# Keeping 21 more rows of x in SBUF between the two passes of a channel-attention kernel

## The chip, the core and the metric

The kernel runs on one core of a Trainium2 chip. A core has TensorE (PE in the profile: matrix products), VectorE (DVE: element-wise work), ScalarE (ACT), GpSimd (POOL) and SyncE (SP), each with an instruction queue of its own. They share SBUF, the on-chip memory with 128 partitions, and PSUM, a small memory into which TensorE writes. Transfers between the chip's main memory (HBM) and SBUF are carried by 16 DMA engines. An engine issues a transfer from its queue and goes on; whoever needs the data waits on a semaphore.

The metric is the device time of one execution in microseconds. Before the change the median of three runs was 741.14 us (741.08 to 743.83).

## What is computed

The input `x` has 384 x 384 pixels with 384 channels in bfloat16, 113.2 MB. Every channel gets one factor, and the factor depends on all pixels:

```python
gap = jnp.mean(xf, 1)                 # xf: pixels x channels
gmp = jnp.amax(xf, 1)
h_a = relu(gap @ w1)                  # w1: 384 x 96
h_m = relu(gmp @ w1)
scale = sigmoid(h_a @ w2 + h_m @ w2)  # w2: 96 x 384
return x * scale                      # one factor per channel
```

So all of `x` has to be read before the first output can be made. What of `x` does not stay on the chip between the two passes has to be read a second time.

## The kernel before

**Rows.** The code counts `x` in rows. One row is one pixel on each of the 128 partitions: 128 x 384 x 2 bytes = 98,304 bytes, or 768 bytes per partition. There are 1152 rows (`TOT`). A block of n rows is n consecutive pixels per partition, so a transfer moves n x 768 consecutive bytes for each partition.

**Where rows live.** SBUF holds six slots of 44 rows (`SLOTS`, L17, tiles `x0` to `x5`) and an 11-row tile `acc`. Between the passes these rows of `x` stay on the chip: the 264 rows in the six slots at the end of the first pass, 16 rows that are copied into PSUM (`kept_ps`, L195) and 2 rows that are copied into another PSUM bank (`kept_b`, L197). The other rows are read again: 859 rows that passed through the slots, and 11 rows (L218, L225) that were loaded beside the 2 kept ones. 264 + 16 + 2 + 859 + 11 = 1152.

**First pass** (the loop at L170). SyncE issues the loads (L174), in the order of the list `loads` (L131 to L139): 16 rows into slot 0 as two transfers of 4 and 12 rows, 13 rows into slot 1, then the 25 blocks of `PASSING` (43, 44, 44, ... down to 13 rows; 859 in all), which go round the six slots beginning with slot 5, then the 264 rows that stay, in the 28 pieces of `STAYING`. That makes 56 transfers. A load into a slot waits until the block before it in that slot has been used by both of its readers. TensorE adds up the channels of each block by products with a column of ones (`sums`, L147). VectorE keeps a running maximum in `acc`, in instructions over 6 and 5 rows in turn (L190). After the first block VectorE copies 16 rows into PSUM (L195), and after the second 2 rows (L197).

**Between the passes.** A short serial chain on all engines folds the sums and maxima, multiplies them with the weights and ends in `scale_bc`, the 384 factors on every partition (L202 to L231).

**Second pass** (the loop at L284). For each block in `order` VectorE multiplies the block by the factors in place (`multiply`, L236) and ScalarE issues the store (L254). First come the six blocks that stayed, the first three of them in small pieces (`FIRST_STORES`), with the two stores of `acc` in between. Once a slot's store has landed, SyncE reads the next of the 20 `again` blocks into it (L263): 19 of 44 rows and, since the list is sorted by size, one of 23 rows at the end. The first two go out as five pieces and one. The two kept blocks come last (L296 to L299): they are multiplied out of PSUM into the slot of the sixth block from the end, and stored.

**Who sets the order.** Each engine works through its queue in order. In the second pass SyncE's order is as written (`manual_schedule`, L282). The order on the other engines is fixed when the program is compiled, by the order of the program text among the instructions whose inputs are there by then. ScalarE's queue is in that order too, so a store cannot overtake the one before it on that queue.

Of the kernel before, what the change touches and what calls it, by code (L numbers as in the profile page):

```python
# [11 lines left out]
BF16 = mybir.dt.bfloat16  # L12
# [3 lines left out]

SLOTS = (44, 44, 44, 44, 44, 44)  # L17
PSUM_ROWS = 16
BANK_ROWS = 2

FIRST_LOAD = 4
# [1 line left out]
ACC_ROWS = 11  # L23

PASSING = (
    43, 44, 44, 43, 43, 44, 43, 42, 42, 39, 38, 37, 36, 36, 35, 34, 32, 29, 29, 27, 27, 23, 21, 15, 13,
)
STAYING = (
    (19, 17, 8), (18, 16, 10), (16, 14, 14), (13, 11, 11, 9), (10, 9, 9, 8, 8), (6, 6, 5, 5, 5, 4, 4, 3, 3, 3),
)  # L30

FIRST_STORES = ((1, 2, 3, 4, 4, 6, 8, 8, 8), (8, 8, 9, 9, 10), (10, 12, 22))

# [9 lines left out]
def kernel(  # L43
# [7 lines left out]
    nc = tc.nc  # L51
    P = nc.NUM_PARTITIONS
    B_, H, W, C = x.shape
# [5 lines left out]
    NS = len(SLOTS)  # L59
# [3 lines left out]
    orr = out.rearrange("b h w c -> (b h w) c")  # L63

    def rows_of(ap, first, n):

        return ap[first * P:(first + n) * P, :].rearrange("(p n) c -> p n c", n=n)
# [4 lines left out]


    beside = BANK_ROWS + A
    head = PSUM_ROWS + beside
    n_stay = sum(SLOTS)
    n_pass = TOT - head - n_stay
    assert sum(PASSING) == n_pass
    stay = []
    for i, n in enumerate(SLOTS):  # L80
        stay.append([head + n_pass + sum(SLOTS[:i]), n, i])
    again = [(head, n_pass % SLOTS[0])] + [
        (head + n_pass % SLOTS[0] + SLOTS[0] * i, SLOTS[0]) for i in range(n_pass // SLOTS[0])
    ]


    small = consts.tile([P, 16], BF16)
# [20 lines left out]
    ]  # L108
    nc.scalar.activation(out=scale_bc[0:1, 0:1], in_=pick[0:1, 0:1], func=ACT.Sigmoid)  # L109
    acc = consts.tile([P, A, C], BF16)  # L110
    slots = [xpool.tile([P, n, C], BF16, name=f"x{s}") for s, n in enumerate(SLOTS)]


    bank_a = psum.tile([P, 512], F32)
    bank_b = psum.tile([P, 512], F32)
    kept_ps = psum.tile([P, PSUM_ROWS, C], BF16)
    sum_ps = bank_a[0:NQP, 0:MM_ROWS * P]
# [6 lines left out]
    z_ps = bank_a[:, 512 - C:512]  # L124
    kept_b = bank_b[:, 0:C * BANK_ROWS // 2].bitcast(BF16).rearrange("p (n c) -> p n c", n=BANK_ROWS)
    gsum_ps = bank_b[:, C:C + CQ]
# [1 line left out]

    loads = [(0, PSUM_ROWS, 0, 0, PSUM_ROWS), (PSUM_ROWS, beside, 1, 0, beside)]  # L131
    done = head
    for i, n in enumerate(PASSING):
        loads.append((done, n, (i - len(PASSING)) % NS, 0, n))
# [8 lines left out]
    def sums(rows, n, done, total):  # L143
        for k in range(0, n, MM_ROWS):
            g = min(MM_ROWS, n - k)
            for q in range(CQ):
                nc.tensor.matmul(  # L147
                    sum_ps[q * QP:q * QP + 1, 0:g * P],
                    lhsT=ones_bf[:, 0:1],
                    rhs=rows[:, k:k + g, q * P:(q + 1) * P],  # L150
                    start=(done + k == 0),
                    stop=(done + k + g == total),
                )

    def turn_sums():

        for r in range(MM_ROWS):
            nc.scalar.copy(out=s_sb[r % 2], in_=sum_ps[:, r * P:(r + 1) * P])  # L158
            nc.tensor.matmul(gsum_ps, lhsT=s_sb[r % 2], rhs=pick, start=(r == 0), stop=False)  # L159

    def tail_sums(rows, n, last):
        for k in range(n):
            for q in range(CQ):
                nc.tensor.matmul(  # L164
                    gsum_ps[:, q:q + 1], lhsT=rows[:, k, q * P:(q + 1) * P], rhs=ones_bf,
                    start=False, stop=(last and k == n - 1 and q == CQ - 1),
                )

    done = turn = 0
    for i, (first, n, s, lo, hi) in enumerate(loads):  # L170
        rows = slots[s][:, lo:hi, :]
        m = hi - lo
        for a, b in ((0, FIRST_LOAD), (FIRST_LOAD, m)) if i == 0 else ((0, m),):
            nc.sync.dma_start(out=rows[:, a:b, :], in_=rows_of(xr, first, n)[:, lo + a:lo + b, :])  # L174
        if i < n_loads - SUM_TAIL:
            sums(rows, m, done, TOT - tail_rows)
        else:
            tail_sums(rows, m, i == n_loads - 1)
        done += m
        if i == n_loads - SUM_TAIL - 1:  # L180
            turn_sums()
        if i == 0:
            nc.vector.tensor_copy(out=acc, in_=rows[:, 0:A, :])  # L183
            lo = A
        j = 0 if i else A
        while j < m:
            c, e = ACC_PARTS[turn]
            turn = (turn + 1) % len(ACC_PARTS)
            e = min(e, c + m - j)
            nc.vector.tensor_tensor(  # L190
                out=acc[:, c:e, :], in0=acc[:, c:e, :], in1=rows[:, j:j + e - c, :], op=ALU.max
            )
            j += e - c
        if i == 0:
            nc.vector.tensor_copy(out=kept_ps.bitcast(U32), in_=rows.bitcast(U32))  # L195
        elif i == 1:
            nc.vector.tensor_copy(out=kept_b.bitcast(U32), in_=rows[:, 0:BANK_ROWS, :].bitcast(U32))  # L197

# [7 lines left out]
    def acc_rows(ap, lo, hi):  # L206
        return rows_of(ap, PSUM_ROWS, beside)[:, BANK_ROWS + lo:BANK_ROWS + hi, :]

    n = A
    acc_pieces = []  # L210
    while n > 1:
# [5 lines left out]
        lo, hi = n, acc_pieces[0][0] if acc_pieces else A  # L217
        nc.sync.dma_start(out=acc[:, lo:hi, :], in_=acc_rows(xr, lo, hi))  # L218
        acc_pieces.append((lo, hi))
    for q0, part in tp_ps:  # L220
        n = part.shape[1]
# [12 lines left out]
    def multiply(dst, src):  # L234
        n = dst.shape[1]
        nc.vector.tensor_tensor(  # L236
            out=dst, in0=src, in1=scale_bc.unsqueeze(1).to_broadcast([P, n, C]), op=ALU.mult
        )
# [52 lines left out]
            read_into(order[k - 1][2])  # L291
    in_order.close()
    assert not again
    s = order[-NS][2]
    n = PSUM_ROWS + BANK_ROWS
    multiply(slots[s][:, 0:PSUM_ROWS, :], kept_ps)  # L296
    nc.scalar.dma_start(out=rows_of(orr, 0, PSUM_ROWS), in_=slots[s][:, 0:PSUM_ROWS, :])
    multiply(slots[s][:, PSUM_ROWS:n, :], kept_b)
    nc.scalar.dma_start(out=rows_of(orr, PSUM_ROWS, beside)[:, 0:BANK_ROWS, :], in_=slots[s][:, PSUM_ROWS:n, :])  # L299
# [28 lines left out]
```

## Time and profile before

| What | Value |
|---|---|
| median of the runs | 741.14 us (741.08, 741.14, 743.83) |
| span of the profiled execution | 743.3 us |
| bytes read and written | 198.92 MB and 113.25 MB |
| mean rate over the span | 420 GB/s |
| VectorE busy | 490.1 us (66%) |
| TensorE busy | 131.4 us (18%) |
| ScalarE and GpSimd busy | 3.3 us and 0.7 us |
| first pass, to the last maximum over x | to 270.7 us |
| first multiplication of the second pass | at 276.3 us |
| last instruction of VectorE | at 706.1 us |

The only time that is given for the profiled execution is its span, from the first to the last instruction; it lies 2.2 us (0.3%) above the median and within the three runs. A page of a profile shows busy time by engine, the span in 40 slices of 18.6 us, the DMA queues, the chain of waits that ended last, and groups of like instructions with what ended the idle time before them. DMA queue q1 carries what SyncE issues, q10 what ScalarE issues.

### The profile page before, as it was taken

Reading aid. Unit: us, or ns where it says so; the run is one execution under the profiler, and the core shown is the slowest. Engines: PE = TensorE matmul, PEld = TensorE weight load, DVE = VectorE, ACT = ScalarE, POOL = GpSimd, SP = SyncE. Lnnn points to the kernel's source line nnn. Section 1 sums busy time; section 2 is a strip of 40 time slices with the busy share of each in tenths; the row PEclk is TensorE's granted clock in tenths of the full one; section 3 lists DMA queues with packets and bytes.
Section 4 is the critical chain, followed back from the end, with each engine's and each line's share of the span. In section 5 each row is a group of like instructions: output and inputs, shape, how many; then the busy total and the mean of one; then the engine's idle time right before and its main releaser. Section 6 shows DMA issues by size and latency. Waiting matters only on the chain.

```text
span 743.3 us, 2595 instructions
## 1 busy us (share of the span) xinstructions
PE 131.4 (18%) x969; PEld 41.7 (6%) x969; DVE 490.1 (66%) x285; ACT 3.3 (0%) x9; POOL 0.7 (0%) x6
## 2 busy tenths in 40 slices
PE   1554445454544540000000000000000000000000
PEld 0111111111111120000000000000000000000000
DVE  5889999999999989998444433434444444433600
ACT  0000000000000000000000000000000000000000
POOL 0000000000000000000000000000000000000000
PEclk9866565567555555555555555555555555555555
DMA  9999999999999979999999999999999999999997
GB/s 381 436 427 432 432 428 431 424 424 438 417 426 420 414 256 376 427 433 433 433 429 435 435 429 433 433 435 435 429 429 429 435 433 436 435 435 427 425 435 310
DMA packets 18812, 312.33 MB, mean 420 GB/s; under 512 B 2448, under 2 KB 3056, under 8 KB 8304
## 3 DMA queue, kind: packets, MB, share of 16 engines
q1 hardware_dynamic: 12464, 198.92, 63.1%
q10 hardware_dynamic: 6336, 113.25, 35.7%
q8 instruction: 7, 0.11, 0.1%
q14 instruction: 5, 0.04, 0.0%
HBM read 198.92 MB, written 113.25 MB: 420 GB/s over the span
## 4 chain that ended last, share of the span: by engine, by line
another core or an unknown queue 40%; DMA 37%; DVE 15%; DVEq 1%; SPq 1%; issue 1%; PE 0%; ACT 0%; ACTq 0%
DMA x<-in_x_dram 31%; DVE acc L190 11%; DMA out_dram<-x 7%; DVE x L236 2%; DVEq L323 1%; SPq L263 1%; DVE kept_ps L195 0%; DVE acc L213 0%; DVE acc L236 0%; DVE acc L183 0%; PE bank_a L230 0%; ACT scale_bc L231 0%; SPq L174 0%; DVE bank_b L197 0%
## 5 line engine op out<-in xcount | busy, mean ns | idle before, releaser
L236 DVE TENSOR_TENSOR x<-x,scale_bc 128x16896 bf16<-128x16896 bf16 (+11 forms) x40 | 229.1, 5769 | 196.4 <-DMA x<-in_x_dram 195.2
L190 DVE TENSOR_TENSOR acc<-acc,x 128x2304 bf16<-128x2304 bf16 (+5 forms) x225 | 245.9, 1166 | 12.8 <-DMA x<-in_x_dram 12.6
L147 PE MATMUL bank_a<-x,small 128*1 128x512 bf16 (+3 forms) x912 | 126.6, 584 | 140.7 <-DMA x<-in_x_dram 140.7
L147 PEld LDWEIGHTS <-small 128*1 128x1 bf16 x912 | 37.8, 112 | 229.1 <-issue 227.6
L183 DVE COPY acc<-x 128x4224 bf16<-128x4224 bf16 x1 | 1.3, 1260 | 5.4 <-DMA x<-in_x_dram 5.4
L195 DVE COPY kept_ps<-x 128x3072 uint32<-128x3072 uint32 x1 | 3.4, 3354 | 0.0
L236 DVE TENSOR_TENSOR x<-kept_ps,scale_bc 128x6144 bf16<-128x6144 bf16 x1 | 3.4, 3351 | 0.0
L213 DVE TENSOR_TENSOR acc<-acc 128x384 bf16<-128x384 bf16 (+2 forms) x4 | 2.6, 658 | 0.1
L236 DVE TENSOR_TENSOR acc<-acc,scale_bc 128x1920 bf16<-128x1920 bf16 (+1 forms) x2 | 2.4, 1250 | 0.0
L158 ACT COPY w_sb<-bank_a 65x128 f32<-65x128 f32 x2 | 0.5, 262 | 265.7 <-PE bank_a L147 265.1
L164 PEld LDWEIGHTS <-x 128*128 128x128 bf16 x39 | 1.3, 109 | 0.0
L109 ACT ACT_TABLE_LOAD x1 | 1.3, 1283 | 0.7 <-PEq L312 0.7
L159 PE MATMUL bank_b<-small,w_sb 65*128 65x3 f32 x4 | 1.2, 365 | 0.4 <-ACT w_sb L158 0.4
L164 PE MATMUL bank_b<-small,x 128*128 128x1 bf16 x39 | 1.2, 165 | 0.0
L159 PE MATMUL bank_b<-small,scale_bc 65*128 65x3 f32 x4 | 1.1, 353 | 0.0
L159 PEld LDWEIGHTS bank_b<-small,w_sb 65*128 65x128 f32 x4 | 1.0, 313 | 0.9 <-ACT w_sb L158 0.9
L159 PEld LDWEIGHTS bank_b<-small,scale_bc 65*128 65x128 f32 x4 | 1.1, 323 | 0.0
L224 DVE TENSOR_REDUCE small<-bank_a 128x2 bf16<-128x256 bf16 x1 | 0.4, 427 | 0.6 <-PE bank_b L223 0.6
L223 PE MATMUL bank_a<-ident_bf,acc 128*128 128x128 bf16 x2 | 0.4, 300 | 1.8 <-DVE acc L213 1.8
L92 DVE MEMSET small<- 128x1 bf16 x1 | 0.1, 59 | 0.8 <-PEq L312 0.8
L118 DVE MEMSET bank_a<- 128x512 f32 x1 | 0.5, 485 | 0.1
L197 DVE COPY bank_b<-x 128x384 uint32<-128x384 uint32 x1 | 0.6, 554 | 0.0
(24 smaller groups left out, 6.3 us busy)
## 6 DMA issues: line engine op xcount, KB each, us to landing
out_dram<-x ACTq DMA_DIRECT2D x22, 4224.0 KB, 79.8
x<-in_x_dram SPq DMA_DIRECT2D x21, 4224.0 KB, 29.2
x<-in_x_dram SPq DMA_DIRECT2D x4, 4128.0 KB, 39.2
x<-in_x_dram SPq DMA_DIRECT2D x2, 4032.0 KB, 49.9
x<-in_x_dram SPq DMA_DIRECT2D x2, 3456.0 KB, 44.2
x<-in_x_dram SPq DMA_DIRECT2D x2, 2784.0 KB, 38.1
x<-in_x_dram SPq DMA_DIRECT2D x2, 2592.0 KB, 35.5
x<-in_x_dram SPq DMA_DIRECT2D x6, 768.0 KB, 16.0
```

The lines of the kernel that those rows point to most:

```text
L109: nc.scalar.activation(out=scale_bc[0:1, 0:1], in_=pick[0:1, 0:1], func=ACT.Sigmoid)
L147: nc.tensor.matmul(sum_ps[q * QP:q * QP + 1, 0:g * P], lhsT=ones_bf[:, 0:1], rhs=rows[:, k:k + g, q * P:(q + 1) * P], start=(done + k == 0 ...
L159: nc.tensor.matmul(gsum_ps, lhsT=s_sb[r % 2], rhs=pick, start=(r == 0), stop=False)
L164: nc.tensor.matmul(gsum_ps[:, q:q + 1], lhsT=rows[:, k, q * P:(q + 1) * P], rhs=ones_bf, start=False, stop=(last and k == n - 1 and q == C ...
L183: nc.vector.tensor_copy(out=acc, in_=rows[:, 0:A, :])
L190: nc.vector.tensor_tensor(out=acc[:, c:e, :], in0=acc[:, c:e, :], in1=rows[:, j:j + e - c, :], op=ALU.max)
L195: nc.vector.tensor_copy(out=kept_ps.bitcast(U32), in_=rows.bitcast(U32))
L197: nc.vector.tensor_copy(out=kept_b.bitcast(U32), in_=rows[:, 0:BANK_ROWS, :].bitcast(U32))
L213: nc.vector.tensor_tensor(out=acc[:, 0:h, :], in0=acc[:, 0:h, :], in1=acc[:, n - h:n, :], op=ALU.max)
L236: nc.vector.tensor_tensor(out=dst, in0=src, in1=scale_bc.unsqueeze(1).to_broadcast([P, n, C]), op=ALU.mult)
L263: nc.sync.dma_start(out=slots[s][:, j:j + m, :], in_=rows_of(xr, first, n)[:, j:j + m, :])
L323: with _tile.TileContext(nc) as tc:
```

## The change

[...] No transfer in this program is issued by GpSimd. [...]

- `held` is loaded as the third load of the first pass, summed and maximised like any block, and stays there.
- One block of 21 rows leaves `PASSING`, which now has 24 blocks and 838 rows. With 24 blocks the round through the slots begins at slot 0, and so the first two loads (16 and 13 rows) move from slots 0 and 1 to slots 4 and 5.
- The rows that are read again are now 18 blocks of 44 rows and two of 23 (`AGAIN`), still 20 blocks.
- After the second pass's loop `held` is multiplied in place and stored, ahead of the two blocks kept in PSUM.

```diff
+RING_BYTES = 256
+HELD_ROWS = 21
 PASSING = (
-    43, 44, 44, 43, 43, 44, 43, 42, 42, 39, 38, 37, 36, 36, 35, 34, 32, 29, 29, 27, 27, 23, 21, 15, 13,
+    43, 44, 44, 43, 43, 44, 43, 42, 42, 39, 38, 37, 36, 36, 35, 34, 32, 29, 29, 27, 27, 23, 15, 13,
 )
+AGAIN = (44,) * 18 + (23, 23)
...
-    head = PSUM_ROWS + beside
+    held_at = PSUM_ROWS + beside
+    head = held_at + HELD_ROWS
...
-    again = [(head, n_pass % SLOTS[0])] + [
-        (head + n_pass % SLOTS[0] + SLOTS[0] * i, SLOTS[0]) for i in range(n_pass // SLOTS[0])
-    ]
+    assert sum(AGAIN) == n_pass
+    again = [(head + sum(AGAIN[:i]), n) for i, n in enumerate(AGAIN)]
...
+    nc.dynamic_dma_scratch_size = RING_BYTES
+    nc.lookup_mloc("DynamicDMAScratchLoc").dims = [P, RING_BYTES]
+    held = nc.alloc_sbuf_tensor_at("held", [P, HELD_ROWS, C], BF16, offset=RING_BYTES).ap()
...
-    loads = [(0, PSUM_ROWS, 0, 0, PSUM_ROWS), (PSUM_ROWS, beside, 1, 0, beside)]
+    bufs = [*slots, held]
+    loads = [
+        (0, PSUM_ROWS, NS - 2, 0, PSUM_ROWS), (PSUM_ROWS, beside, NS - 1, 0, beside), (held_at, HELD_ROWS, NS, 0, HELD_ROWS),
+    ]
...
-        rows = slots[s][:, lo:hi, :]
+        rows = bufs[s][:, lo:hi, :]
...
     assert not again
+    multiply(held, held)
+    nc.scalar.dma_start(out=rows_of(orr, held_at, HELD_ROWS), in_=held)
```

## The prediction

> **What bounds the kernel now.** I read the page's head and slices first, then the DMA queues, the stretches of the two passes, the chain of waits and the waits of SyncE's queue. In the page, busy time comes before the slices:
>
> ```profile
> span 743.3 us, 2595 instructions
> ...
> PE 131.4 (18%) x969; PEld 41.7 (6%) x969; DVE 490.1 (66%) x285; ACT 3.3 (0%) x9; POOL 0.7 (0%) x6
> ...
> DVE  5889999999999989998444433434444444433600
> ...
> DMA  9999999999999979999999999999999999999997
> GB/s 381 436 427 432 432 428 431 424 424 438 417 426 420 414 256 376 427 433 433 433 429 435 435 429 433 433 435 435 429 429 429 435 433 436 435 435 427 425 435 310
> ```
>
> No engine is busy all the time, but the transfers are: 9 in every slice except at the boundary of the passes (slice 15) and at the end. The rate is the same for reads alone (slices 2 to 14), reads and writes together (17 to 36) and writes alone (38, 39). So the kernel is bound by bytes, whichever way they go. The queues:
>
> ```profile
> q1 hardware_dynamic: 12464, 198.92, 63.1%
> q10 hardware_dynamic: 6336, 113.25, 35.7%
> q8 instruction: 7, 0.11, 0.1%
> q14 instruction: 5, 0.04, 0.0%
> HBM read 198.92 MB, written 113.25 MB: 420 GB/s over the span
> ```
>
> All data go through two hardware queues, and there is no queue of GpSimd's. Stretches of the span (columns: window, its length, busy us of PE, PEld, DVE, ACT, POOL, clock of PE, DMA share, GB/s):
>
> ```profile
> 20.00:100.00 80.00, 37.37 (x267) 11.26 (x264) 74.33 (x65) 0.00 (x0) 0.00 (x0) 0.68 1.01 433
> ...
> 240.00:262.00 22.00, 11.95 (x90) 3.27 (x84) 21.82 (x23) 0.00 (x0) 0.00 (x0) 0.50 1.01 413
> ...
> 270.00:278.00 8.00, 2.44 (x36) 1.64 (x33) 5.88 (x13) 0.83 (x3) 0.00 (x0) 0.50 0.60 166
> ...
> 292.00:335.00 43.00, 0.00 (x0) 0.00 (x0) 43.00 (x10) 0.00 (x0) 0.00 (x0) 0.50 1.02 418
> 335.00:660.00 325.00, 0.00 (x0) 0.00 (x0) 149.97 (x17) 0.00 (x0) 0.00 (x0) 0.50 1.00 432
> ...
> 698.00:733.00 35.00, 0.00 (x0) 0.00 (x0) 8.49 (x3) 0.00 (x0) 0.00 (x0) 0.50 0.99 426
> ```
>
> In the second pass VectorE works less than half the time (150.0 of 325 us) beside full queues. The chain in order of time shows a beat there; "unknown queue" is the store that SyncE waits for:
>
> ```profile
> 371.10 0.33 SPq L263
> 371.43 19.54 another core or an unknown queue
> ...
> 651.85 0.33 SPq L263
> ```
>
> From 371.10 to 651.85 SyncE issues 14 times more: (651.85 - 371.10) / 14 = 20.05 us for 44 rows read and 44 written, 0.2279 us a row. That is my price for a row.
>
> The first pass is less clear. VectorE is busy there for nearly all of it (250.86 of the first 270 us), and SyncE waits for it:
>
> ```profile
> SPq L263 <- DMA out_dram<-x: 379.0, 20, 21.8
> SPq L174 <- DVE acc L190: 178.7, 24, 11.4
> ```
>
> But those are waits of the issuer, not of the engines that move data: loads of 42 to 44 rows land 29 to 50 us after their issue, and even the 3-row ones 8.5 us after. A queue with that much ahead of a new load is not empty.
>
> **The change, part by part.**
>
> *Second pass, reads.* 859 rows become 838: 21 rows fewer, 2.06 MB. At 0.2279 us a row that is 4.79 us. Bounds: 4.76 at the 434 GB/s between 660 and 698 us, 4.94 at the 418 between 292 and 335. I take 4.79, from the stage in which the bytes are saved. It counts in full because stores wait behind: with fewer reads the same engines drain q10 sooner. SyncE's 24 issues in this pass stay 24, since the blocks stay 20.
>
> [...]
>
> *Second pass, VectorE.* One block of 44 rows (8956 ns) becomes one of 23 (4759 ns), and a multiplication of 21 rows is added; the nearest row is the 22-row one (4547 ns), so about 4.34 us. Net: -4.20 + 4.34 = +0.14 us, hidden: VectorE waits 188.7 us for re-read blocks. Where it stands in VectorE's queue is settled at compile time: after the last block, as written, or in the first wait, at about 351 us, because `held` is ready by then. If late, 4.76 + 4.34 + 3.35 + 0.55 = 13.0 us of VectorE work follow the last re-read block, 8.7 before. Behind VectorE's end at 706 us stores still run until about 741, so 35 us cover 4.3. If early, it fills an idle time of 8.99 us, and its store is 4.8 us of traffic between others on a queue that is never empty. Without that cover the price would be 4.3 us, which is the whole gain.
>
> *Second pass, ScalarE's queue.* One store issue more (45 for 44, 0.34 us as at L297), behind the same cover: 0. The copies kept in PSUM wait for the store of the sixth block from the end. About four blocks of stores are in flight (a 44-row store lands 79.8 us after its issue, four beats), so that store has landed by then, with two blocks of 23 at the end as well.
>
> *First pass, bytes and issues.* 1152 rows and 56 transfers, as before: 0.
>
> *First pass, the start.* Loads 1 to 3 have 16, 13 and 21 rows, not 16, 13 and 43. VectorE is done with the first two at 15.97 us, then waits 3.94 us for the 43 rows, which begin at 19.92. The 21 rows land 22 x 0.2279 = 5.0 us earlier, at 14.9; VectorE takes them at once until 15.97 + 21 x 0.2148 (9.44 us for 44 rows) = 20.5; the next 43 land at 19.92 + 21 x 0.2279 = 24.7. It waits 4.2 us, so 0.26 more than now. Bounds 0 (transfers set the pass) and +0.26 (VectorE sets it); the traces of both are there, so half, +0.13. SyncE gets further ahead: slots 0 to 3 are free from the beginning, and the copy to PSUM (3.35 us, done at 11.6) now holds back the eighth load, not the fourth.
>
> *First pass, the end.* The last six blocks before the staying ones held 27+27+23+21+15+13 = 126 rows, and now 29+27+27+23+15+13 = 134. So the loads that stay find 134 rows ahead of them at most (30.5 us), not 126 (28.7). If the dip to 413 GB/s at 240 to 262 us came from an empty queue, this could win up to 22 x (433 - 413) / 433 = 1.0 us; since 3-row loads still land 8 us after issue, I think the short pieces cause it, and take 0.
>
> *Between the passes* nothing changes: `held` can't be stored before the factors exist, so the 5.6 us from 270.7 to 276.3 stay.
>
> *The sum.* -4.79 + 0.13 = -4.66 us on the profiled execution: 743.3 to 738.6. The profiled one is 2.2 us above the median of the runs; against the median, 741.14 - 4.66 = 736.5 us, or -0.63%.
>
> [...]
>
> **The rivals.** About 0.5% (3.7 us) is what a measurement of this kernel can tell from no change.
>
> *The rate slips.* The re-read blocks begin at other rows of `x` (50 + 44k, was 52 + 44k). The rate of the slices in the second pass goes from 427 to 436 without a cause that I can see. At 1% less over the 422 us from 288 to 710, 4.2 us go and the time is 740.7. It takes only 0.2% (0.9 us) to bring the gain under 0.5%. Against it: the beats before, at fourteen different places in `x`, all last 19.9 to 20.5 us. Same, mostly.
>
> *VectorE sets the first pass.* With 251 of 270 us busy it has 19 us of slack. If one more wait like the 3.94 us arises in the round that was shifted by a slot, most of the gain is gone: 736.5 + 3.9 = 740.4. Against it: the waits after the fourth load are 0.8, 1.9 and 0.4 us, since each block lands shortly before or after VectorE is ready. Same.
>
> [...]
>
> *More is gained:* the 1.0 us at the end of the first pass, and 4.94 for the rows: 735.2.
>
> **How the numbers follow.** Forecast 0.77 (own range 735.4 to 737.4: the bounds of rate and start, and half a microsecond of spread), more gained 0.03, the rate slips 0.11 (0.09 same, 0.02 slower), VectorE 0.04 (same), the ring 0.05 (slower). Faster by over 0.5% (under 737.4): 0.77 + 0.03 = 0.80. Same: 0.13. Slower: 0.07. The range goes from 735.2, all bounds on the good side, to 739.2, where the rate has slipped by 0.65%; it leaves out the ring and the worse half of the other two.
>
> **What would show it.** In the profile after: q1 at 196.85 MB and q10 unchanged; the beat still 20.0 us; the pass boundary (end of the last maximum over x) within 0.3 us of 270.7; VectorE's first long wait 4.2 us at about 20.5; the last re-read block landing some 5 us earlier than 698, stores running on to the end without a gap. Wrong: a rate under 428 GB/s between 335 and 660 us; idle DMA slices outside slices 15, 16 and 40; a first pass that ends after 272 us; a `held` multiplication that waits, or behind which the last stores wait with an empty queue.

## The result and the profile after

The changed kernel takes 737.38 us (median of 736.69, 737.25, 737.52 and 737.92), the kernel before 741.15 us beside it. The ratio is 0.9943 with a 95% interval of 0.9927 to 0.996: 4.2 us less, between 3.0 and 5.4. The forecast was 736.5 us, a ratio of 0.9937.

The head, the slices and the queues of the page after:

```profile
span 736.1 us, 2598 instructions
...
DVE  6789999999999989999444464444444444445400
...
GB/s 382 438 431 435 423 433 423 431 426 431 423 427 418 417 277 370 415 423 438 425 435 439 432 428 435 437 433 428 435 437 433 428 435 437 433 424 436 436 428 346
...
q1 hardware_dynamic: 12464, 196.86, 63.0%
q10 hardware_dynamic: 6480, 113.25, 36.1%
...
HBM read 196.85 MB, written 113.25 MB: 421 GB/s over the span
```

The read queue carries 2.06 MB less, which is 21 rows; the write queue carries the same. The mean rate is the one from before (421 beside 420 GB/s), and it dips in the same slices.

The spans of the two profiles, 743.3 and 736.1 us, differ by 7.2 us, and that is not what the change did. The profiled execution of the kernel before was a long one. The time of a run is 1.7 to 1.9 us above the span of the same execution (737.92 us beside 736.1), so by an estimate from this difference a span of 743.3 us belongs to a run of about 745 us: above all runs of the kernel before, not within them. Its beats of the second pass grew from 19.9 us at 371 us to 20.5 us near the end (start, length, what):

```profile
371.10 0.33 SPq L263
391.03 0.33 SPq L263
...
631.39 0.33 SPq L263
651.85 0.33 SPq L263
```

A better partner is the profile of a kernel that reads all rows like the one before and differs from it only in one size, that of the ring (the first experiment below; its median is 1.0004 times that of the kernel before). Here is its chain of waits in order of time, at the first and last of fifteen issues, fourteen beats apart:

```profile
371.42 0.33 SPq L265
...
650.92 0.33 SPq L265
```

And the chain of the changed kernel:

```profile
372.24 0.33 SPq L273
...
651.66 0.33 SPq L273
```

Fourteen beats take 279.50 and 279.42 us, so 19.96 us each in both: a row costs 19.96 / 88 = 0.2268 us, and 21 rows 4.76 us. From the first of these beats to the end of the span it is 740.1 - 371.4 = 368.7 us without held rows and 736.1 - 372.2 = 363.9 us with them. The difference is 4.8 us, which is the price of the 21 rows. The whole spans differ by 4.0 us, because the stretch ahead of the first beat took 0.8 us longer in this execution; such differences come up again in the last section.

What happened to the held rows is in the list of instructions that touch `held`:

```profile
L200 DVE TENSOR_TENSOR acc<-acc,held x4: 950/1250/1352, 15.7 to 19.3; 128x2304 bf16<-128x2304 bf16 x2, 128x1920 bf16<-128x1920 bf16 x1, 128x1536 bf16<-128x1536 bf16 x1
L184 SPq DMA_DIRECT2D held<-in_x_dram x1: 432/432/432, 2.1 to 2.1; - x1
L246 DVE TENSOR_TENSOR held<-held,scale_bc x1: 4351/4351/4351, 428.7 to 428.7; 128x8064 bf16<-128x8064 bf16 x1
L305 ACTq DMA_DIRECT2D out_dram<-held x1: 617/617/617, 695.1 to 695.1; - x1
```

Their load is issued at 2.1 us, and they are in the maximum by 20.2 us, since the last of four instructions starts at 19.3 us (the numbers after the colon are shortest, median and longest ns, then first and last start in us). The multiplication has been moved into a wait of VectorE at 428.7 us, and the wait after it is the shorter for it, 6.73 us where those around it are 11.0 us:

```profile
439.79 8.96 DVE L246 TENSOR_TENSOR x<-x,scale_bc 128x16896 bf16<-128x16896 bf16 x1 [6.73 <-DMA x<-in_x_dram]
```

The store stayed where the program has it, behind the last block's store in ScalarE's queue, 266 us later.

The start of VectorE's timeline (start, length, engine, line, operation; the wait ahead of it in brackets):

```profile
15.20 0.56 DVE L207 COPY bank_b<-x 128x384 uint32<-128x384 uint32 x1
15.67 4.55 DVE L200 TENSOR_TENSOR acc<-acc,held 128x2304 bf16<-128x2304 bf16 x4
24.47 9.24 DVE L200 TENSOR_TENSOR acc<-acc,x 128x2304 bf16<-128x2304 bf16 x8 [4.25 <-DMA x<-in_x_dram]
...
270.32 2.74 DVE L223 TENSOR_TENSOR acc<-acc 128x1920 bf16<-128x1920 bf16 x4
```

VectorE does not wait for the held rows; its longest wait after the one for the very first rows is still that for the first big block, 4.25 us (3.94 before). The first pass ends at 270.3 us (270.8 before).

### The profile page after: what moved, and what is told of

It reads as the page before. It is cut to its first block, busy times and chain, and to the rows that moved or that the text cites. A ratio compares the mean times of both kernels' runs of the same rounds, so it can differ in the third digit from the quotient of the medians.

```text
span 736.1 us, 2598 instructions
## 1 busy us (share of the span) xinstructions
PE 128.1 (17%) x969; PEld 41.1 (6%) x969; DVE 490.2 (67%) x286; ACT 3.3 (0%) x9; POOL 0.7 (0%) x6
## 4 chain that ended last, share of the span: by engine, by line
another core or an unknown queue 39%; DMA 39%; DVE 13%; DVEq 1%; SPq 1%; issue 1%; PE 0%; ACT 0%; ACTq 0%
DMA x<-in_x_dram 32%; DVE acc L200 10%; DMA out_dram<-x 7%; DVE x L246 2%; DVEq L335 1%; SPq L273 1%; SPq L184 0%; DVE acc L223 0%; DVE acc L246 0%; PE bank_a L240 0%; ACT scale_bc L241 0%; DVE small L234 0%; PE bank_a L233 0%; PE bank_a L238 0%
## 5 line engine op out<-in xcount | busy, mean ns | idle before, releaser
L246 DVE TENSOR_TENSOR x<-x,scale_bc 128x16896 bf16<-128x16896 bf16 (+11 forms) x40 | 224.9, 5665 | 188.6 <-DMA x<-in_x_dram 187.4
L200 DVE TENSOR_TENSOR acc<-acc,x 128x2304 bf16<-128x2304 bf16 (+5 forms) x221 | 241.4, 1167 | 12.6 <-DMA x<-in_x_dram 12.3
L157 PE MATMUL bank_a<-x,small 128*1 128x512 bf16 (+3 forms) x894 | 120.9, 571 | 140.4 <-DMA x<-in_x_dram 140.4
L200 DVE TENSOR_TENSOR acc<-acc,held 128x2304 bf16<-128x2304 bf16 (+2 forms) x4 | 4.6, 1201 | 0.0
L246 DVE TENSOR_TENSOR held<-held,scale_bc 128x8064 bf16<-128x8064 bf16 x1 | 4.4, 4351 | 0.0
L157 PE MATMUL bank_a<-held,small 128*1 128x512 bf16 (+1 forms) x18 | 2.4, 570 | 3.2 <-DMA held<-in_x_dram 3.2
## 6 DMA issues: line engine op xcount, KB each, us to landing
x<-in_x_dram SPq DMA_DIRECT2D x2, 2784.0 KB, 38.1
```

The lines of the kernel that those rows point to most:

```text
L157: nc.tensor.matmul(sum_ps[q * QP:q * QP + 1, 0:g * P], lhsT=ones_bf[:, 0:1], rhs=rows[:, k:k + g, q * P:(q + 1) * P], start=(done + k == 0 ...
L200: nc.vector.tensor_tensor(out=acc[:, c:e, :], in0=acc[:, c:e, :], in1=rows[:, j:j + e - c, :], op=ALU.max)
L246: nc.vector.tensor_tensor(out=dst, in0=src, in1=scale_bc.unsqueeze(1).to_broadcast([P, n, C]), op=ALU.mult)
```

## The experiments

The theory to test: the gain is 0.227 us for each row that is not read again, and nothing else in the change has a price. Each ratio is to the kernel before, run on the same chip beside the experiment.

### The ring alone

`RING_BYTES` in the code of the change is the size that the change gives to a region of the program, the ring in what follows; `held` begins at that byte of each partition. Here the size is set as in the change, no tensor is laid behind it, and all rows are read as in the kernel before.

```diff
     acc = consts.tile([P, A, C], BF16)
+    nc.dynamic_dma_scratch_size = 256
+    nc.lookup_mloc("DynamicDMAScratchLoc").dims = [P, 256]
```

> [...] Theory (the gain is the bytes that are not read again, and the ring has no user): ratio to before 1.000, within 0.15% either way (740 to 742 us). Rival (the hardware queues lean on the ring, or its size has an effect by itself): a ratio off by more than 0.3%, up or down.

Measured: 741.9 us, ratio 1.0004 (0.9995 to 1.0013). By the interval the smaller size costs between -0.4 and 1.0 us, so no price of it shows. To a slower kernel because of the ring the prediction had given 0.05.

### The first pass alone

The 21 rows take their own buffer in the first pass but are read again in the second. The output is complete.

```diff
-AGAIN = (44,) * 18 + (23, 23)
+AGAIN = (23,) + (44,) * 19
...
-    again = [(head + sum(AGAIN[:i]), n) for i, n in enumerate(AGAIN)]
+    again = [(held_at + sum(AGAIN[:i]), n) for i, n in enumerate(AGAIN)]
...
-    multiply(held, held)
-    nc.scalar.dma_start(out=rows_of(orr, held_at, HELD_ROWS), in_=held)
```

> The 21 rows go through their own buffer as third load, and the first pass is that of the change, with its shifted round of the slots; in the second pass these rows are read again like the others, as one block of 23 and 19 of 44 rows, the same blocks as before. Theory: the first pass is set by its transfers, so ratio 1.000, +0.1 us as the working has it, 741.3 us. Rival (the order of the first pass is a part of the gain or eats some of it): at least 1 us off, 740 or 742.

Measured: 742.19 us, ratio 1.0001 (0.9992 to 1.0009). The shifted round through the slots and the smaller third load are worth less than can be measured, 0.7 us at most either way by the interval. The gain lies in the second pass.

### Fewer rows, and the change once more

For 10 rows:

```diff
-HELD_ROWS = 21
+HELD_ROWS = 10
...
-    43, 44, 44, 43, 43, 44, 43, 42, 42, 39, 38, 37, 36, 36, 35, 34, 32, 29, 29, 27, 27, 23, 15, 13,
+    43, 44, 44, 43, 43, 44, 43, 42, 42, 39, 38, 37, 36, 36, 35, 34, 32, 29, 29, 27, 27, 23, 11, 15, 13,
...
-AGAIN = (44,) * 18 + (23, 23)
+AGAIN = (44,) * 18 + (28, 29)
```

> 10 rows are held instead of 21; one passing block of 21 rows becomes one of 11, and the last two blocks that are read again have 28 and 29 rows. Theory (0.227 us for each row that is not read again): -2.3 us, ratio 0.9969, 738.9 us. Rival (the gain comes from the new order, not from the bytes): the same as with 21 rows, 737.4, or the same as before, 741.1.

> The changed kernel once more, with more rounds, beside the others. Theory: 21 rows at 0.227 us are 4.76 us, so ratio 0.9936, 736.4 us. The first comparison gave 0.9943, about 0.5 us less than that. Rival (something eats a part of the gain, such as a lower rate of the transfers in the second pass): 0.9945 or more, and an interval that leaves 0.9936 out.

Measured: 10 rows 739.81 us, 0.997 (0.9959 to 0.9981), or 2.2 us less; 21 rows 737.45 us, 0.994 (0.9928 to 0.9953), or 4.5 us less. That is 0.22 and 0.21 us a row. The interval of the second holds 0.9936, so nothing is known to eat a part of the gain; the 0.3 us that the middle of it falls short by can't be told from no difference with this many runs.

### Where the blocks begin, where the store stands, when the rows are loaded

Three variants of the change, each with one detail put elsewhere. The two blocks of 23 rows are taken from the front of the rows that are read again (they are still read last), so that the blocks of 44 rows begin where they did before:

```diff
-AGAIN = (44,) * 18 + (23, 23)
+AGAIN = (23, 23) + (44,) * 18
```

> The change, with the two blocks of 23 rows taken from the front of the re-read rows: the 18 blocks of 44 rows then begin at the same rows of x as in the kernel before. Theory: where a block begins does not matter, so the same as the change, ratio 0.994 (0.9936 by the price of a row). Rival (the shift of the blocks by two rows costs some of the rate): 0.5 us or more faster than the change, ratio 0.993 or less.

The held rows' multiplication and store after the sixth block:

```diff
         k += 1
+        if k == NS:
+            multiply(held, held)
+            nc.scalar.dma_start(out=rows_of(orr, held_at, HELD_ROWS), in_=held)
         if k == LEAD:
...
-    multiply(held, held)
-    nc.scalar.dma_start(out=rows_of(orr, held_at, HELD_ROWS), in_=held)
```

> The multiplication of the held rows and their store come right after the six blocks that stayed in the slots, no longer at the end. Theory: the store is 4.8 us of traffic wherever it stands on a queue that never runs empty, so ratio 0.994 as with the change. Rival (it delays the reads, which wait for the stores ahead of them): up to 4.8 us slower, ratio 1.000. Other rival (the long run of stores alone at the end has a lower rate): faster by 0.5 us or more, 0.993 or less.

The held rows loaded late:

```diff
     loads = [
-        (0, PSUM_ROWS, NS - 2, 0, PSUM_ROWS), (PSUM_ROWS, beside, NS - 1, 0, beside), (held_at, HELD_ROWS, NS, 0, HELD_ROWS),
+        (0, PSUM_ROWS, NS - 2, 0, PSUM_ROWS), (PSUM_ROWS, beside, NS - 1, 0, beside),
     ]
...
     for i, n in enumerate(PASSING):
+        if i == len(PASSING) - 2:
+            loads.append((held_at, HELD_ROWS, NS, 0, HELD_ROWS))
         loads.append((done, n, (i - len(PASSING)) % NS, 0, n))
```

> The held rows are loaded where the 21-row block stood before, between the blocks of 23 and 15 rows, not third. Theory: the gain does not depend on when they come, so ratio 0.994, within 0.3 us of the change. Rival (the early third load gives VectorE a better start): about the 0.3 us that separate the waits, not to be told apart; a result 1 us or more slower would mean that the order carries a part of the gain.

All three together:

> The change with the three variants together that came out level or a little ahead of it: the held rows loaded late, their store after the sixth block, the two blocks of 23 rows taken from the front. If the differences (0.3 to 1.0 thousandths) were real and add up: ratio 0.992 or less, 735 us. If they are the spread of the measurement: 0.9936, as the price of a row has it.

| Variant | us | ratio | 95% interval |
|---|---|---|---|
| blocks begin as before | 736.77 | 0.9937 | 0.9923 to 0.9951 |
| store after the sixth block | 737.01 | 0.9934 | 0.9921 to 0.9947 |
| held rows loaded late | 736.98 | 0.993 | 0.9916 to 0.9944 |
| all three | 738.0 | 0.9944 | 0.9932 to 0.9956 |

None can be told from the change, and the three together are not faster, so the small differences between them were spread. The early store shows best why it made no difference here. The held rows' store is issued at 337.1 us and lands 68.6 us later. Here it is with the beats around its landing, from the chain of waits:

```profile
L299 ACTq DMA_DIRECT2D out_dram<-held x1: 338/338/338, 337.1 to 337.1; - x1
...
391.02 0.33 SPq L273
391.34 28.13 another core or an unknown queue
...
419.54 0.33 SPq L273
419.86 15.77 another core or an unknown queue
...
435.69 0.33 SPq L273
```

Two beats take 435.69 - 391.02 = 44.67 us instead of 2 x 19.96 = 39.92. The store costs its 4.75 us here, and these 4.75 us are no longer at the end: from its first beat at 371.1 us to the end of its span at 735.0 it is 363.9 us again.

### More and less of VectorE's work in the first pass

The prediction had left open whether VectorE or the transfers set the end of the first pass. In three variants VectorE repeats the maximum over the 23-row block (index 24 of `loads`, at about 200 us), repeats the one over the held rows (index 2, at 20 us), or leaves out the one over the 23-row block. Repeating a maximum changes nothing in the result; the third variant leaves these 23 rows out of the maximum.

```diff
+        for _ in range(2 if i == 24 else 1):     # 2 if i == 2: early; 0 if i == 24: left out
             j = 0 if i else A
             while j < m:
                 ...
```

> The change, with the maximum over the 23-row block of the first pass taken twice, at about 200 us: 23 x 0.215 = 4.9 us more of VectorE's work in four or five instructions, which leave the result as it is. From 180 to 270 us VectorE waits only 0.9 us. If VectorE sets the end of the first pass together with the transfers: 4.9 - 0.9 = 4 us slower than the change, ratio 0.9994. If the transfers alone set it, as most of the working assumed: no more than 0.5 us slower, ratio 0.9945.

> The change, with the maximum over the held rows taken twice, at 20 us: 4.55 us more of VectorE's work, just ahead of its longest wait (4.25 us) and of further waits of 0.3 to 2.1 us. If VectorE's work costs nothing where transfers are late and everything where they are not: the same as the change, ratio 0.994. If any work of VectorE in the first pass comes out at its end: 4 us slower, 0.9995 as with the 23-row block.

> The change, with the maximum over the 23-row block of the first pass left out (so these rows are missing from the maximum): 4.9 us less of VectorE's work at about 200 us. If VectorE alone sets the end of the first pass: 4 us faster than the change, ratio 0.9885. If it and the transfers are even there (the last load lands at about 269.5 us, VectorE's last maximum over x ends at 270.7): no more than 1 us faster, 0.9925 to 0.994.

| Variant | us | ratio | 95% interval | fold of `acc` begins |
|---|---|---|---|---|
| late, 4.9 us more | 741.33 | 0.9993 | 0.9985 to 1.0002 | 274.45 us |
| early, 4.55 us more | 737.73 | 0.9941 | 0.9928 to 0.9954 | 270.61 us |
| late, 4.9 us less | 739.59 | 0.9974 | 0.9956 to 0.9992 | 270.87 us |

The end of VectorE's timeline in the first pass, in the repeat of the change:

```profile
196.34 35.63 DVE L200 TENSOR_TENSOR acc<-acc,x 128x2304 bf16<-128x2304 bf16 x34 [0.32 <-DMA x<-in_x_dram]
232.18 38.54 DVE L200 TENSOR_TENSOR acc<-acc,x 128x2304 bf16<-128x2304 bf16 x39 [0.21 <-DMA x<-in_x_dram]
```

with the late addition:

```profile
183.53 12.12 DVE L201 TENSOR_TENSOR acc<-acc,x 128x1920 bf16<-128x1920 bf16 x11 [0.17 <-DMA x<-in_x_dram]
195.89 76.52 DVE L201 TENSOR_TENSOR acc<-acc,x 128x2304 bf16<-128x2304 bf16 x76 [0.25 <-DMA x<-in_x_dram]
...
274.45 2.73 DVE L224 TENSOR_TENSOR acc<-acc 128x1920 bf16<-128x1920 bf16 x4
```

and with that maximum left out:

```profile
195.94 5.83 DVE L201 TENSOR_TENSOR acc<-acc,x 128x2304 bf16<-128x2304 bf16 x5 [0.33 <-DMA x<-in_x_dram]
205.17 6.10 DVE L201 TENSOR_TENSOR acc<-acc,x 128x1920 bf16<-128x1920 bf16 x6 [3.40 <-DMA x<-in_x_dram]
212.56 9.58 DVE L201 TENSOR_TENSOR acc<-acc,x 128x1920 bf16<-128x1920 bf16 x10 [1.28 <-DMA x<-in_x_dram]
222.53 9.51 DVE L201 TENSOR_TENSOR acc<-acc,x 128x1920 bf16<-128x1920 bf16 x9 [0.39 <-DMA x<-in_x_dram]
232.27 38.56 DVE L201 TENSOR_TENSOR acc<-acc,x 128x2304 bf16<-128x2304 bf16 x39 [0.24 <-DMA x<-in_x_dram]
```

With more work VectorE runs from 195.9 us on without a wait and ends 3.7 us later than in the repeat of the change (270.75), and the time is 741.33 us, 3.9 us above the 737.45 of that repeat. With less work it waits 3.40, 1.28 and 0.39 us for loads instead and ends at 270.87 us, 0.1 us from where it ended in the repeat. So neither alone sets the end of the first pass here: 4.9 us of work more move it by 3.7 us, 4.9 us less by 0.1. By an estimate from the waits that VectorE has left after 196 us in the repeat (0.32 and 0.21 us), transfers and VectorE arrive within about half a microsecond of each other. Early in the pass 4.55 us more are taken up by the wait of 4.25 us, which is gone here, and by those after it, and the fold begins at 270.61 us:

```profile
15.94 9.03 DVE L201 TENSOR_TENSOR acc<-acc,held 128x2304 bf16<-128x2304 bf16 x8
24.89 9.24 DVE L201 TENSOR_TENSOR acc<-acc,x 128x2304 bf16<-128x2304 bf16 x8
34.77 9.44 DVE L201 TENSOR_TENSOR acc<-acc,x 128x2304 bf16<-128x2304 bf16 x8 [0.65 <-DMA x<-in_x_dram]
```

The time with less work, 739.6 us, is not explained by that: both expectations had it level with the change or faster, and it is 2.4 us slower. Its runs go from 738.06 to 743.47 us, three of nine at 742.0 or more, while the profiled one (738.68) has the same first pass and the same beats of 19.96 us as the change. I don't know what made the long ones long, and read only the place of the boundary from this kernel.

### How much the stores cover at the end

```diff
             rows = slots[s][:, j:j + m, :]
+            if k == len(order) - 1:
+                for _ in range(8):
+                    nc.vector.tensor_tensor(out=rows, in0=rows, in1=rows, op=ALU.max)
             multiply(rows, rows)
```

> The change, with eight more passes of VectorE over the last block that is read again (the maximum of the block with itself, 4.76 us each, which changes nothing), 38.1 us in all ahead of its multiplication. Theory (the stores behind cover VectorE's late work): the store of that block could be issued as late as 733 - 62 rows x 0.227 = 719 us without loss, and is issued at about 694.5; so 24 us are covered and 14 us come out, 751 us, ratio 1.013. Rival (no cover at the end): all 38 us, ratio 1.045.

Measured: 754.2 us, ratio 1.0167 (1.015 to 1.0183). Against the 0.994 of the change that is 0.0227 x 742.0 = 16.8 us, so 38.1 - 16.8 = 21.3 us of the added work were covered. In stretches of its span (window, length, busy us of PE, PEld, DVE, ACT, POOL, clock, DMA share, GB/s) the queue can be seen to run dry (0 GB/s from 726 to 738 us):

```profile
690.00:716.00 26.00, 0.00 (x0) 0.00 (x0) 25.04 (x7) 0.00 (x0) 0.00 (x0) 0.50 0.99 425
716.00:726.00 10.00, 0.00 (x0) 0.00 (x0) 9.93 (x3) 0.00 (x0) 0.00 (x0) 0.50 0.29 124
726.00:738.00 12.00, 0.00 (x0) 0.00 (x0) 11.40 (x3) 0.00 (x0) 0.00 (x0) 0.50 0.00 0
738.00:754.10 16.10, 0.00 (x0) 0.00 (x0) 0.00 (x0) 0.00 (x0) 0.00 (x0) 0.50 0.90 379
```

The older stores last to about 719 us, as expected. The 2.8 us more than the expected 14 fit VectorE's timeline: the two kept blocks (3.35 and 0.55 us) were multiplied in between, ahead of the last block's own multiplication, which came at 732.71 us. With them, 42.0 us of work were put ahead of that multiplication and 25 us covered, near the expected 24:

```profile
690.89 4.76 DVE L265 TENSOR_TENSOR x<-x 128x8832 bf16<-128x8832 bf16 x1 [10.42 <-DMA x<-in_x_dram]
695.56 3.35 DVE L246 TENSOR_TENSOR x<-kept_ps,scale_bc 128x6144 bf16<-128x6144 bf16 x1
698.83 4.75 DVE L265 TENSOR_TENSOR x<-x 128x8832 bf16<-128x8832 bf16 x1
703.50 0.55 DVE L246 TENSOR_TENSOR x<-bank_b,scale_bc 128x768 bf16<-128x768 bf16 x1
703.96 28.71 DVE L265 TENSOR_TENSOR x<-x 128x8832 bf16<-128x8832 bf16 x6
732.71 4.76 DVE L246 TENSOR_TENSOR x<-x,scale_bc 128x8832 bf16<-128x8832 bf16 x1
```

The last block's store could so be issued at 737.5 us, 18.5 us after the 719 us; the span of this execution, 754.1 us, is 18.0 us above that of the change.

## Why the prediction was right, point by point

**The reads of the second pass (-4.79 us): right.** The term is 4.8 us from the beats on, and 10 rows gain in proportion. The price per row was a little high, 0.2279 for 0.2268 us, because it was taken from the growing beats of a long execution. That the saving counts in full holds in the runs: with the held rows' store at the end or after the sixth block, the stretch from the first beat to the end was 363.9 us, beside 368.7 without held rows. The prediction gave the stores that wait behind as the reason; no run takes them away, so that stays its argument.

**The start of the first pass (+0.13 us): the wait was right, the term should have been 0.** VectorE took the held rows at 15.67 us, waited 4.25 us (4.2 expected) and got the next block at 24.47 us (24.7). But 4.55 us more of work at that place did not move the boundary (270.61 us beside 270.75): a lateness this early was lost in the waits that follow. Halving between the bounds was a way not to decide; the three short waits between 29 and 52 us (0.8, 1.9 and 0.4 us), which the text itself names against a rival, are more than the 0.26 us and would have decided it.

**VectorE's slack in the first pass: wrong.** The rival gave VectorE 19 us of slack, 270 less 251 us of busy time. That is the slack of the whole pass. In the part that counts, from about 196 us on, it is about 1 us at most: the waits there add up to 0.5 us, and 4.9 us more of work cost 3.7 us at the boundary. The sentence on queues that are not empty is right for the transfers (a DMA share of 1.00 from 60 to 200 us and 0.98 from 200 to 270 in the repeat of the change) and says nothing about VectorE, which was even with them. That the forecast took no harm from this is luck as far as this argument goes: the change adds no work late in the pass.

**The end of the first pass (0, at best 1.0 us): right.** With 134 rows ahead of the staying loads instead of 126, the rate from 240 to 262 us is 413 GB/s as before, so eight more rows in the queue did not lift the dip. The stretch in the changed kernel (columns as above):

```profile
240.00:262.00 22.00, 12.00 (x87) 3.35 (x89) 21.82 (x23) 0.00 (x0) 0.00 (x0) 0.50 1.01 413
```

**The held multiplication: hidden, as forecast, but not where.** It came at 428.7 us, not at 351 or at the end, and its store did not follow it but stayed behind that of the last block. The cover at the end was put at 35 us; 21 to 25 us were there. The 35 us reach from VectorE's end to the end of the stores, and the stores that can only go out after VectorE's last block (62 rows, 14.1 us, the held rows among them because their store stands behind it in ScalarE's queue) must not be counted as cover for it.

**The ring, and the place of the blocks in x: no loss from either.** That the ring slows the kernel, for which the prediction has 0.05, no run shows: with its size alone the ratio is 1.0004 (0.9995 to 1.0013), and the change with `held` behind it gains its 4.8 us from the first beat on. Blocks that begin as before give 0.9937 beside 0.994. The rate did not slip: the steady beat is 19.96 us with the ring alone and with the change.

**Against which time, and the range:** the sum of -4.66 us was set against a profiled execution of 743.3 us. Beside the two kernels that read everything again, profiled at 740.1 and 740.4 us, the change's 736.1 and 735.7 lie 4.0 to 4.7 us lower. The median that was measured, 737.38, is 0.9 us above the forecast, which is within the interval of the ratio. The inner range, 735.4 to 737.4 us, is 0.3 us wider on each side than the bounds it names add up to (735.7 to 737.1); nothing hangs on it.

## What to carry to other kernels

Here the transfers ran at nearly one rate from end to end (421 GB/s over the span, 19.96 us a beat), 21 rows that were not read again were worth their time at that rate (4.8 us, 0.2268 us a row), and the order around them made no difference that could be measured (0.993 to 0.9944 for the change and four variants of its order): take the price from the steady beat, and check that the beat is steady first. Slack is to be read in the stage where it would be used: VectorE was idle for 19 us of the first pass and still had about 1 us at most to give in its last 70 us. Work added at the end was covered here only by the traffic that was already in the queue (21 to 25 us of 38 to 42), not by the traffic that it releases itself (from 738 us on, after 12 us at 0 GB/s).

## What was not expected

- Transfers and VectorE end the first pass together. Taking 4.9 us from VectorE's late work gains nothing at the boundary and adding 4.9 us costs 3.7.
- The stretch from the end of the first pass to the first of the steady beats differs from execution to execution of like kernels by over a microsecond: 270.32 to 372.24 us (101.9 us) in the profile of the change, 270.75 to 371.69 (100.9) in its repeat, 270.63 to 370.71 (100.1) with the blocks of 23 rows at the front. It is 100.4 and 101.0 us in the two kernels that read all rows again. From there to the end the three agree to 0.1 us (363.9, 364.0, 363.9). No experiment tells what the difference hangs on.
- The beat itself is steady to 0.1 us in eleven other profiles, the beats beside an early store aside, but grew to 20.5 us in the one of the kernel before, which made that execution 3.5 us longer from the first beat to the end (743.3 - 371.1 = 372.2 us instead of 368.7). The cause stays open.
